# The first slot's first layer, moved from the start of the expert part into the tail of attention

## The chip, the cores and the metric

The kernel runs on one core of a Trainium2 chip. TensorE (PE) multiplies, with PEld as its weight load; VectorE (DVE), ScalarE (ACT) and GpSimd (POOL) do elementwise work, GpSimd also the gathers and scatters by index; SyncE (SP) issues the other transfers. The metric is the time of one execution on the device in microseconds, the median of three runs for the kernel before.

## The reference

Attention over 4 batches and 8 heads of 576 positions with 64 features, causal, mixed by a gate g per head with a read of a memory. Its result, as 2304 tokens of 512 features, goes through a layer of 8 experts, of which each token takes the one with the highest logit:

```
scores = q @ k.T / 8, masked causally;  a = softmax(scores);  local = a @ v
q_p = phi(q);  mem_out = (q_p @ M_prev) / (q_p . z_prev + 1e-6)
x = g * mem_out + (1 - g) * local          # 2304 tokens x 512
e = argmax(x @ w_gate);  w = softmax(x @ w_gate)[e]
out = w * (relu(x @ w1[e]) @ w2[e])        # w1: 512 x 1024, w2: 1024 x 512, 8 experts
```

## The kernel before

**Attention.** The work is cut into 16 units (two heads of a batch each) and every unit into steps: maxima (`n`), scores (`s`), local sums (`p`), the memory read (`m`, `d`), assembling the rows (`a`). Each step has a time in units, from the table `K`, with a shift of its own in `K["sh"]`; `at` and `add` put the steps into a list, the list is sorted by time and the steps are written out in that order (end of `attention`, L944 to L973). A scheduler puts the instructions into each engine's queue from there. The weights of expert 0 and 1 are loaded and cut into two fp16 halves (`Wh`, `Wl`, high and low part, scaled by 64) during attention, each in 8 units of 512 KB. Finished rows go to `x_scratch` in memory, each with its gate value behind it.

**The tail.** When the logits are there, `routing(0)` and `routing(1)` (the steps of `Routing.part`) compute for each token its expert and its rank in it. A slot is 128 tokens of one expert, or half a slot 64; the slots of all experts follow each other, and the table `tab` (TensorE, L1140 and L1155) has for each of them the list of its tokens. `fin1` (L1160, L1161) makes two index tables of it: `idx` for gathers and `ids` for scatters. `busy` (L1067) puts matmuls between the steps whose result nobody reads ("fillers"): four and five of 512 columns, and 46 of 64 columns at the end of `tokens` (`wt`, `wu`, `w3` in `K`). `early_x` gathers the rows of slot 0, which is called the early slot, already in the tail, cuts them into high and low halves and turns them into `rout.xT`.

**The experts.** All engines meet (L1838) and enter a part whose order and semaphores are written by hand. POOL issues the gather of slot 1 (L1490, semaphore `g0`), SP issues the eight loads of the next expert to be staged (L1384), TensorE computes the early slot's first layer (`first_part`, L1582: two halves of 48 matmuls, into the PSUM tiles `m_ph`) and then its second layer (`second_part`, L1598). The rows of slot 1 are cut on VectorE (L1761, L1763), turned on TensorE (L1671) and copied by ScalarE (L1726) and VectorE (L1769). From slot 2 on the rows are turned by SP with transposing transfers: `xtrans` (L1411) issues two of them, for the high and the low half, and VectorE copies the result (L1794). After that the engines run loops over experts and slots: blocks `F0` to `F2` (whole slots) and `H0` to `H2` (half slots) on TensorE, `act_body` and `dve_body` beside them; the weights of later experts are loaded and cut in between. The counts that decide the loops come from VectorE (L1171 to L1177, semaphore `cn`).

The lines of SP at the start of the experts:

```
for u in range(8):
    load(1, u)
...
SP.wait_ge(S["cn"], 7)
...
    SP.dma_start_transpose(out=xB[:, j], in_=xn[j])   # xtrans, after waits for xc, xh, xl
```

Of the kernel before, what the change touches and what calls it, by code (L numbers as in the profile page):

```python
# [17 lines left out]
K = dict(wa=(6, 0, 2, 0, 0, 1, 1, 1, 1, 1, 2, 0, 3, 0, 1, 1, 1, 1, 0, 0, 1, 0, 0), d=3.648, wt=4, wu=5, wv=0, w3=46,  # L18
         sz=(2.207, 2.265, 2.085, 2.03), cr=-1.987, cast1=-0.91, tk1=-0.345, phi0=0.603, pt0=1.592, x0=(19.192,
         19.398), s0=(1.627, 2.3), s1=(1.023, 1.757), p0=(1.742, 3.247), n1=(-0.782, -1.174), n2=(0.27, 0.743),  # L20
         p1=(1.918, 3.326), wd=(8, 8), nc1=0, pact=11, wact=0, pact1=2, wact1=0, nc3=0, cuts=((1, 2), (0, 0)),
         rc=7.857, r0=(15.971, 18.058), r1=(19.098, 21.477), ap=(17.292, 17.456), al=(17.639, 18.974), at=(19.203,
         20.025), k1=-1.514, setup=1.819, v1=2.195, sw=(2.949, 3.089, 3.067, 3.361), sm=(3.958, 3.522, 3.566),
         cast=-0.886, castd=0.004, tk=-0.422, tq=-0.437, phi=0.504, pt=2.11, lk=-1.843, lq=-1.872, lv=0.681,
         n=(-0.15, 0.75), s=(1.05, 2.002), p=(2.014, 3.031), m0=(4.286, 4.261), m7=(2.592, 3.425), m=(2.535, 3.7),
         a0=(4.4, 4.897), a=(4, 5.2), wl=(14.447, 14.278, 15.631, 16.029, 16.835, 17.2, 17.2, 17.976), wc=(15.676,
         17.041, 15.78, 17.231, 17.473, 16.982, 18.21, 17.972), sh=dict(m_steps1w=0.41, wconv01=0.05,
         s_steps14w=0.24, a_steps4=1.03, const_q1=2.08, n_first68=0.16, first_q2=0.12, m_steps2w=0.08,
         p_steps2w=0.15, wload03=-0.02, wconv03=-1.21, s_first12=0.52, setup=-0.73, n_steps4=-0.15, s_steps6w=-0.51,
         p_steps0=0.1, s_steps13=-0.07, phi21=1.31, wload06=0.31, s_steps8w=0.79, wload10=0.62, load6k=-0.33,  # L30
         s_steps4=-0.04, setup_w0=-0.1, n_steps15=-0.7, n_steps13=0.15, n_steps2w=-0.23, load5q=0.27,
# [1193 lines left out]
def experts(nc, tc, es, x_dram, mem, rout, w1, w2, out):  # L1225
# [29 lines left out]
    with tc.tile_critical():  # L1255
# [165 lines left out]
        for u in range(8):  # L1421
            load(1, u)
# [419 lines left out]
```

## Time and profile before

| | kernel before |
|---|---|
| median of three runs | 496.48 us (496.2 to 498.18) |
| the profiled execution, its own time | 493.86 us |
| its span, first to last instruction | 492.1 us |
| granted TensorE clock, mean (1 is 2.4 GHz, 0.5 is 1.2 GHz) | 0.988 |
| TensorE busy, matmuls | 459.1 us (93%) |
| VectorE, ScalarE, GpSimd busy | 355.0, 221.3, 213.4 us |
| chain that ended last, by engine | PE 64%, DVE 12%, SP's queue 8%, DMA 6%, issue 5% |

The three runs and the profiled execution are different executions: durations are read from the profiled one, and a sum over them is compared with its 493.86. In the profile's rows the line is that of the source; "out<-in" are the buffers; a bracket behind a row gives how long the engine stood idle ahead of it and what ended that. In the windows "0.30 (x5)" is busy time with the number of instructions. "issue" is time in which an engine waited for nothing that the profile shows.

### The profile page before, as it was taken

The page shows a single profiled execution, that of the slowest core. Times are in us where ns is not written, and L with a number is a line of the kernel's source. Part 1 is how long each engine was busy: PE and PEld are TensorE (multiplying, and loading weights), DVE is VectorE, ACT ScalarE, POOL GpSimd, SP SyncE. Part 2 cuts the span into 40 slices and gives each one's busy share as a digit, 9 for nine tenths or more (in the row PEclk, how much of TensorE's full clock was granted, in tenths as well). Part 3 has the DMA queues.
Part 4 walks back from the last instruction along what each step waited for, and adds up shares of the span by engine and source line. Part 5 has one row for each costly group of instructions (what it writes and reads, how often), then busy time and mean ns, then how long its engine had stood idle before and what let it go on. Part 6 is the DMA issues. An engine that isn't in the chain of part 4 may idle for free.

```text
span 492.1 us, 14309 instructions
## 1 busy us (share of the span) xinstructions
PE 459.1 (93%) x5279; PEld 314.1 (64%) x5280; DVE 355.0 (72%) x785; ACT 221.3 (45%) x361; POOL 213.4 (43%) x396
## 2 busy tenths in 40 slices
PE   2999899999999989999978999999999989999885
PEld 1555456666666646657656777676677767777864
DVE  2788489786869647989885778788843489844682
ACT  3788565556666655457610444433300163300701
POOL 6567657367748344656331423132232122232132
PEclk9999799999999999999989999999999999999999
DMA  5667979999899989885247999799973199963232
GB/s 119 137 119 158 182 158 172 174 193 228 175 161 164 272 164 191 183 177 209 65 135 286 253 332 254 231 261 305 274 182 98 45 256 304 318 139 90 57 73 69
DMA packets 170106, 90.57 MB, mean 184 GB/s; under 512 B 151471, under 2 KB 152751, under 8 KB 170032
## 3 DMA queue, kind: packets, MB, share of 16 engines
q1 hardware_dynamic: 166192, 77.95, 67.8%
q0 software_dynamic: 3840, 11.80, 7.8%
q8 instruction: 26, 0.43, 0.3%
q14 instruction: 48, 0.39, 0.3%
HBM read 55.35 MB, written 11.60 MB: 136 GB/s over the span
## 4 chain that ended last, share of the span: by engine, by line
PE 64%; DVE 12%; SPq 8%; DMA 6%; issue 5%; ACT 2%; POOL 1%; DVEq 1%; POOLq 0%; ACTq 0%
PE m_ph L1582 18%; PE m_py L1598 16%; PE o L565 7%; PE st L491 5%; SPq L275 3%; PE loc L677 3%; PE sm L596 3%; PE sn L404 2%; SPq L277 2%; DMA m_xB<-m_xn 2%; DMA QT<-mem 1%; DVE mem L1276 1%; PE wm L882 1%; DVE m_w L1276 1%; PE sn L421 1%
## 5 line engine op out<-in xcount | busy, mean ns | idle before, releaser
L1582 PEld LDWEIGHTS m_ph<-m_xT,mem 128*128 128x128 f16 x1344 | 66.0, 98 | 5.9 <-issue 3.3
L1582 PE MATMUL m_ph<-m_xT,mem 128*128 128x128 f16 (+1 forms) x1344 | 67.1, 212 | 2.6 <-DVE m_xT L1794 2.6
L1711 ACT ACTIVATE m_y<-m_py 128x512 f32<-128x512 f32 x17 | 10.2, 597 | 121.6 <-PE m_py L1598 121.6
L510 ACT ACTIVATE aT<-st 128x512 f32<-128x512 f32 x96 | 55.2, 594 | 17.6 <-PE st L491 17.1
L412 DVE TENSOR_REDUCE mt<-sn 128x1 f32<-128x512 f32 (+4 forms) x83 | 54.2, 663 | 12.2 <-PE sn L410 10.0
L495 POOL TENSOR_SCALAR_AFFINE_SELECT aT<-aT 128x128 f32<-128x128 f32 (+2 forms) x160 | 48.0, 317 | 31.9 <-ACT aT L510 29.9
L1598 PE MATMUL m_py<-mem,m_hT 128*128 128x512 f16 x264 | 58.9, 379 | 1.8 <-DVE m_hT L1751 1.8
L565 PE MATMUL o<-aT,mem 128*64 128x320 f32 (+4 forms) x320 | 59.2, 433 | 0.0
L1751 DVE TENSOR_SCALAR m_hT<-m_ph 128x512 f16<-128x512 f32 (+1 forms) x46 | 29.0, 631 | 38.5 <-PE m_ph L1582 37.3
L1538 POOL COPY m_ig<-r_idx 128x1 int32 x22 | 4.0, 184 | 112.9 <-DVE m_xn L1783 111.8
L491 PE MATMUL st<-mem 128*128 128x64 f16 (+6 forms) x224 | 46.8, 262 | 0.4 <-ACT aL L532 0.2
L1598 PEld LDWEIGHTS m_py<-mem,m_hT 128*128 128x128 f16 x264 | 25.3, 98 | 30.3 <-issue 2.0
L491 PEld LDWEIGHTS <-mem 128*128 128x128 f16 (+1 forms) x448 | 32.9, 99 | 16.3 <-issue 4.4
L1582 PEld LDWEIGHTS m_ph<-m_xT,m_w 128*128 128x128 f16 x768 | 40.9, 98 | 3.1 <-issue 1.1
L491 PE MATMUL st<-QT,mem 66*128 66x64 f16 (+6 forms) x224 | 42.3, 262 | 0.4 <-ACT QT L455 0.4
L1582 PE MATMUL m_ph<-m_xT,m_w 128*128 128x128 f16 (+1 forms) x768 | 41.8, 216 | 0.9 <-issue 0.7
L1598 PE MATMUL m_py<-m_w,m_hT 128*128 128x512 f16 x168 | 37.4, 379 | 0.0
L565 PEld LDWEIGHTS o<-aT,mem 128*64 128x64 f32 x320 | 25.3, 137 | 16.7 <-issue 9.8
L1504 POOL DMA_INDIRECT out_dram<-m_y,m_is x23 | 27.2, 1184 | 19.9 <-POOL m_is L1510 19.9
L404 PE MATMUL sn<-mem 128*128 128x128 f16 (+3 forms) x158 | 31.2, 275 | 1.5 <-DVE mt L412 1.1
L1490 POOL DMA_INDIRECT m_xg<-x_scratch,m_ig x22 | 24.0, 1089 | 17.5 <-POOL m_ig L1538 17.5
L1753 DVE SCALAR_TENSOR_TENSOR m_hT<-m_ph,m_hT 128x512 f16<-128x512 f32 (+1 forms) x46 | 29.1, 633 | 1.6
(259 smaller groups left out, 904.2 us busy)
## 6 DMA issues: line engine op xcount, KB each, us to landing
mem<-in_moe_w_dram SPq DMA_DIRECT2D x40, 512.0 KB, 6.1
m_stage<-in_moe_w_dram SPq DMA_DIRECT2D x24, 512.0 KB, 6.6
mem<-in_k_dram SPq DMA_DIRECT2D x32, 128.0 KB, 3.0
mem<-in_q_dram SPq DMA_DIRECT2D x32, 128.0 KB, 2.8
mem<-in_v_dram SPq DMA_DIRECT2D x32, 128.0 KB, 2.8
x_scratch<-xb SPq DMA_DIRECT2D x3, 1152.0 KB, 5.9
mem<-mem SPq DMA_DIRECT2D x6, 288.0 KB, 4.1
x_scratch<-xb SPq DMA_DIRECT2D x1, 864.0 KB, 3.8
```

The costliest lines, as they stand in the source:

```text
L404: nc.tensor.matmul(ps[:, c:c + k1 - k0], QT[:, 5 * hh + t, :], keys(hh)[:, k0:k1], start=(c == 0), stop=(k1 == parts[-1][3] and hh == part ...
L412: nc.vector.reduce_max(out, v, axis=AX.X)
L491: nc.tensor.matmul(ps[:, c:c + n], kk[:, kb, :], qq[:, w:w + n], start=(first and i == 0 and j == 0), stop=(last and i == 1 and j == len(p ...
L495: nc.gpsimd.affine_select(out=ap, in_=ap, pattern=pattern, compare_op=ALU.is_ge, fill=0.0, base=base, channel_multiplier=-1)
L510: nc.scalar.activation(out=a, in_=ps, func=AF.Exp, scale=ESC)
L565: nc.tensor.matmul(o[64 * hh:64 * hh + 64, q0:q0 + n], vv, aa, start=(j == 0), stop=(j == 4), skip_group_check=True)
L1490: G.indirect_dma_start(out=x.rearrange("p h e -> p (h e)"), out_offset=None, in_=x_dram, in_offset=bass.IndirectOffsetOnAxis(ap=i, axis=0) ...
L1504: G.indirect_dma_start(out=out, out_offset=bass.IndirectOffsetOnAxis(ap=i, axis=0), in_=ysb[:, j], in_offset=None, bounds_check=bound, oob ...
L1582: mm = PE.matmul(ph[i2][:, f, 0:N], w[:, kc, c:c + 128], x[:, j, kc, 0:N], start=(i == 0), stop=(i == 11), skip_group_check=True)
L1598: mm = PE.matmul(py, hh, ww[:, 4 + ff // 2, c:c + 512], start=st, stop=sp_)
L1751: V.tensor_scalar(out=hT[i2][0][:, :, 0:N], in0=ph[i2][:, :, 0:N], scalar1=0.0, scalar2=None, op0=ALU.max).then_inc(S[hi], 1)
L1753: V.scalar_tensor_tensor(out=hT[i2][1][:, :, 0:N], in0=ph[i2][:, :, 0:N], scalar=0.0, in1=hT[i2][0][:, :, 0:N], op0=ALU.max, op1=ALU.subtr ...
```

## The change

Slot 0's first layer leaves the expert part and becomes a step `early_p` of attention's list: 24 chunks of four matmuls each, with the times `K["e0"]`. Its result stays in two tiles of a PSUM pool `rout.acc` that both parts now use. At the start of the expert part ScalarE takes the high half (with relu) and VectorE the low half; TensorE goes straight to the second layer. SyncE waits for slot 1's gather before it issues the eight loads. `fin1` makes only one column for that gather and the table `ids`; `idx` is made from it on GpSimd, behind the gather. The 46 fillers go from `tokens` to the start of attention (`fill`), the five at L1144 fall away (`wu=0`), and a block "room" of 48 matmuls is put into TensorE's program, entered only if `er`, which starts at 1, is under 1. `K` gets new times nearly everywhere. The core of the diff:

```diff
-K = dict(wa=(...), d=3.648, wt=4, wu=5, wv=0, w3=46,
-         ... x0=(19.192, 19.398), ... r0=(15.971, 18.058), r1=(19.098, 21.477), ...
+K = dict(wa=(...), d=3.668, wt=4, wu=0, wv=0, w3=46, room=48,
+         ... x0=(19.233, 19.268), e0=(19.944, 21.6), ... r0=(15.971, 18.056), r1=(19.042, 22.191), ...
...
+    def fill(n):
+        for _ in range(n):
+            nc.tensor.matmul(wm[0][:, 0, 0:64], ident16, ident16[:, 0:64], start=True, stop=True)
...
+    at(-1.995, fill, K["w3"])
...
+        def early_p(i):
+            Wh, Wl = W[0]
+            got = []
+
+            def chunk(i2, f, w, j, first, last):
+                def f_():
+                    if first:
+                        got.append(rout.acc.tile([128, 4, 128], F32, tag="acc", name=f"ph{i2}", bufs=2))
+                        rout.ph = got
+                    c = 512 * i2 + 128 * f
+                    for kc in range(4):
+                        nc.tensor.matmul(got[i2][:, f], w[:, kc, c:c + 128], rout.xT[:, j, kc], start=(first and kc == 0),
+                                         stop=(last and kc == 3), skip_group_check=True)
+                return f_
+
+            todo = []
+            for i2 in range(2):
+                q = [(f, w, 0) for f in range(4) for w in (Wh, Wl)] + [(f, Wh, 1) for f in range(4)]
+                todo += [chunk(i2, f, w, j, k == 0, k == 11) for k, (f, w, j) in enumerate(q)]
+            return todo
...
         add(early_x, 0, 4, *K["x0"])
+        add(early_p, 0, 24, *K["e0"])
...
-            busy(K["w3"], 64)
 
         def fin1():
-            V.tensor_scalar(out=s.idx[:, 0:NS], in0=s.tab[0], scalar1=-1.0, scalar2=2304.0, op0=ALU.min, op1=ALU.add)
+            V.tensor_scalar(out=s.i1, in0=s.tab[0][:, 1:2], scalar1=-1.0, scalar2=2304.0, op0=ALU.min, op1=ALU.add)
             V.tensor_scalar(out=s.ids[:, 0:NS], in0=s.tab[0], scalar1=2304.0, scalar2=None, op0=ALU.add)
...
-    ph = [pp.tile([128, 4, 128], F32, name=f"m_ph{i}") for i in range(2)]
+    ph = rout.ph
...
+        SP.wait_ge(S["g0"], 16)
         for u in range(8):
             load(1, u)
...
-        gather("g0", xg0, idx[:, 1:2])
+        gather("g0", xg0, rout.i1)
+        G.tensor_scalar(out=idx, in0=ids, scalar1=2303, scalar2=None, op0=ALU.min).then_inc(S["ix"], 1)
...
+        G.wait_ge(S["ix"], 1)
         G.wait_ge(S["cn"], 7)
...
-        for i2 in range(2):
-            first_part(i2, 128, *W[0], rout.xT).then_inc(S[f"q{i2}"], 1)
         PE.wait_ge(S["q0hi"], 1)
         second_part(0, 0, 0, 128, *W[0])
...
         with block("Z"):
+            PE.br_lt(er, 1, on_true="room", on_false="H0")
+        with block("room"):
+            for _ in range(K["room"]):
+                PE.matmul(py[:, 0:64], rout.ident16, rout.ident16[:, 0:64], start=True, stop=True)
             PE.br("H0")
...
+        for i2 in range(2):
+            A.activation(out=hT[i2][0], in_=ph[i2], func=AF.Relu).then_inc(S[f"q{i2}hi"], 1)
...
-        relu(0, 128, once, "q0hi", "q0lo")
+        for i2 in range(2):
+            V.wait_ge(S[f"q{i2}hi"], 1)
+            V.scalar_tensor_tensor(out=hT[i2][1], in0=ph[i2], scalar=0.0, in1=hT[i2][0],
+                                   op0=ALU.max, op1=ALU.subtract).then_inc(S[f"q{i2}lo"], 1)
```

How the instructions stand, at three places. The first is TensorE's queue in the tail. `r_pr` is the count of the ranks, `r_tab` the table, `r_warm` a filler, `mem_60` the turned rows of the early slot, `mem_59` the weights of expert 0. Before:

```order
L1088 MATMUL r_pr<-r_less,r_ones 128x8
L1088 MATMUL r_pr<-r_ohs,r_ones 128x8
L1067 LDWEIGHTS r_ones
L1067 MATMUL r_warm<-r_ones 128x512
...
L1155 LDWEIGHTS aT
L1155 MATMUL r_tab<-aT 128x144
...
L1067 MATMUL r_warm<-r_ones 128x64
...
L1838 UNCONDITIONAL_BRANCH
L1582 MATMUL m_ph_4122<-mem_60,mem_59 128x128 x48
L1582 MATMUL m_ph_4123<-mem_60,mem_59 128x128 x48
L1598 MATMUL m_py<-mem_59,m_hT_4109 128x512 x8
```

and now:

```order
L1114 MATMUL r_pr<-r_less,r_ones 128x8
L1114 MATMUL r_pr<-r_ohs,r_ones 128x8
L984 LDWEIGHTS mem_59
L984 MATMUL ph_4020<-mem_60,mem_59 128x128
...
L984 MATMUL ph_4113<-mem_60,mem_59 128x128
L1181 LDWEIGHTS aT
L1181 MATMUL r_tab<-aT 128x144
...
L984 LDWEIGHTS mem_59
L984 MATMUL ph_4113<-mem_60,mem_59 128x128
```

The fillers between the counts and the table, and those behind it, are gone; in their places stand matmuls of the early slot's first layer (`ph_4020` is its first half, `ph_4113` its second): 36 between the counts and the table, 28 behind it. 32 more stand ahead of these counts. The two rows of 48 matmuls behind the crossing are no longer there.

The second is POOL's queue from the crossing into the expert part on; `r_idx` and `r_ids` are the index tables, `r_i_70` the new column. Before:

```order
L1838 UNCONDITIONAL_BRANCH
L1490 DMA m_xg_4103<-x_scratch,r_idx 128x576
L1551 TENSOR_LOAD r_cnt
L1552 REGISTER_ALU
L1553 UNCONDITIONAL_BRANCH
L1553 ISA
L1553 COMPARE_AND_BRANCH
L1501 ISA
L1538 COPY m_ig<-r_idx 128x1
```

and now:

```order
L1874 UNCONDITIONAL_BRANCH
L1516 DMA m_xg_4199<-x_scratch,r_i_70 128x576
L1520 TENSOR_SCALAR r_idx<-r_ids 128x145
L1579 TENSOR_LOAD r_cnt
L1580 REGISTER_ALU
L1581 UNCONDITIONAL_BRANCH
L1581 ISA
L1581 COMPARE_AND_BRANCH
```

The table is made directly behind the gather and ahead of the loading of the counts.

The third is VectorE's queue in the maxima of the second unit, early in attention. `sn` are scores in PSUM, `mt` their maxima, `wg_sw` the gating weights in another order, `gm` and `gl` the gates; L436 to L440 before, L435 to L439 after, end the unit's maxima, and the transpose of SyncE for that unit follows them. Before:

```order
L412 TENSOR_REDUCE mt_122<-sn 128x2 x2
L427 TENSOR_REDUCE mt_122<-sn 128x1
L428 TENSOR_REDUCE mt_122<-sn_411 128x1
L412 TENSOR_REDUCE mt_122<-sn 128x1
L181 TENSOR_SCALAR gm<-bt 128x8
L182 TENSOR_SCALAR gl<-bt 128x8
L412 TENSOR_REDUCE mt_122<-sn 128x1
L185 COPY wg_sw<-wg_sb 128x4x7
L186 COPY wg_sw<-wg_sb 128x4
L436 TENSOR_TENSOR mt_122<-mt_122 128x9
```

and now:

```order
L411 TENSOR_REDUCE mt_126<-sn 128x2 x2
L427 TENSOR_REDUCE mt_126<-sn_457 128x1
L184 COPY wg_sw<-wg_sb 128x4x7
L185 COPY wg_sw<-wg_sb 128x4
L191 COPY IW<-wg_sw 64x4x8 x2
L205 COPY early<-wg_sw 64x4x8
L426 TENSOR_REDUCE mt_126<-sn 128x1
L411 TENSOR_REDUCE mt_126<-sn 128x1
L205 COPY early<-wg_sw 64x4x8
```

The copies of the gating weights have moved ahead of maxima which they stood behind.

## Rows read from the trace of the kernel before

**Rows 1.** Windows, two parts: length, busy us (count) by engine, PEclk, DMA share, GB/s

```profile
core 0: us, PE busy (x) PEld busy (x) DVE busy (x) ACT busy (x) POOL busy (x), PEclk, DMA share, GB/s
26.00:246.00 220.00, 212.32 (x2182) 132.00 (x2182) 171.33 (x475) 135.34 (x242) 129.97 (x276) 0.98 0.86 176
246.00:260.00 14.00, 10.03 (x97) 7.02 (x96) 10.66 (x41) 1.98 (x6) 4.23 (x7) 0.88 0.37 120
```

**Rows 2.** Chain that ended last, 240 to 275 us: start, length, engine and line

```profile
254.76 2.04 PE r_warm L1067 x5
256.80 0.60 PE r_tab L1155 x5
257.40 1.82 PE r_warm L1067 x46
259.22 1.33 issue
260.55 5.52 PE m_ph L1582 x96
```

**Rows 3.** Timeline, 236 to 272 us: start, length, engine; idle before in brackets

```profile
260.31 4.03 SPq L1384 DMA_DIRECT2D mem<-in_moe_w_dram  x8
...
260.57 1.03 POOL L1490 DMA_INDIRECT m_xg<-x_scratch,r_idx  x1 [6.63 <-issue]
...
266.81 0.49 DVE L1761 TENSOR_SCALAR m_xn<-m_xg 128x512 f16<-128x512 f32 x1 [1.97 <-DMA m_xg<-x_scratch,r_idx]
...
269.75 0.69 DVE L1769 CAST m_xT<-m_px 128x512 f16<-128x512 f32 x1 [0.34 <-ACT m_xT L1726]
...
271.35 1.24 SPq L1411 DMA_TRANSPOSE m_xB<-m_xn  x1
```

**Rows 4.** DMA issues, the two gathers: queue, count, us from issue to landing

```profile
q<-x_scratch,r_i POOLq DMA_INDIRECT x1, 3.7
m_xg<-x_scratch,r_idx POOLq DMA_INDIRECT x1, 6.2
```

**Rows 5.** Timeline of PE, 271 to 330 us: first layer of slots 1, 2

```profile
271.54 5.52 PE L1582 MATMUL m_ph<-m_xT,mem 128*128 128x128 f16 x96
...
282.08 5.52 PE L1582 MATMUL m_ph<-m_xT,mem 128*128 128x128 f16 x96
```

**Rows 6.** Windows round three holes of PE: before the hole or in it, behind it

```profile
50.00:51.80 1.80, 0.12 (x10) 0.00 (x0) 0.00 (x0) 0.60 (x1) 1.04 (x1) 1.00 0.97 187
...
53.40:60.20 6.80, 6.80 (x29) 2.34 (x29) 3.79 (x4) 4.34 (x6) 5.09 (x4) 0.50 1.06 165
252.70:254.70 2.00, 0.30 (x5) 0.22 (x4) 1.94 (x12) 0.25 (x1) 1.16 (x2) 1.00 0.13 36
254.70:258.20 3.50, 3.50 (x30) 2.21 (x29) 2.31 (x12) 0.90 (x4) 0.00 (x0) 0.51 0.41 105
...
394.00:396.00 2.00, 0.91 (x18) 0.67 (x13) 1.23 (x2) 2.00 (x3) 1.04 (x1) 1.00 0.62 188
```

**Rows 7.** Line L1384, its first eight loads

```profile
DMA to landing us min/median/max: 3.3/7.3/11.2
```

**Rows 8.** DMA packets by size, 271.4 to 273.4 us, then 273.4 to 277

```profile
DMA packets 404, 0.78 MB, mean 391 GB/s; under 512 B 22, under 2 KB 22, under 8 KB 404
...
DMA packets 1308, 0.78 MB, mean 216 GB/s; under 512 B 1121, under 2 KB 1121, under 8 KB 1308
```

**Rows 9.** Windows at the end of the first transposes

```profile
276.50:277.00 0.50, 0.50 (x12) 0.50 (x9) 0.46 (x1) 0.00 (x0) 0.50 (x1) 1.00 0.34 131
```

**Rows 10.** Chain that ended last, 300 to 492 us: a transpose in quiet time

```profile
390.23 1.21 SPq L1411
...
394.77 0.64 DVE m_xT L1794
```

**Rows 11.** Timeline of DVE, 22 to 37 us: a maximum and a copy

```profile
28.34 0.69 DVE L427 TENSOR_REDUCE mt<-sn 128x1 f32<-128x512 f32 x1 [1.01 <-PE sn L426]
...
30.86 1.18 DVE L185 COPY wg_sw<-wg_sb 128x28 f32<-128x28 f32 x1
```

**Rows 12.** Timeline of PE, 301 to 321 us: a stop inside an expert block

```profile
318.83 1.57 PE L1582 MATMUL m_ph<-m_xT,m_w 128*128 128x128 f16 x25 [0.71 <-issue]
```

More of the change, by code (lines that the diff above doesn't have):

```diff
@@ L73 @@
 SW = 64.0
 emitted = []
-TUNE = ["r1", "at", "ap", "al", "x0"]
+TUNE = ["r1", "at", "ap", "al", "x0", "e0"]
 def weight_unit(w1, w2, p, u):
@@ L549, in start @@
         def start():
-            T["o", u] = ps_1.tile([128, 512], F32, tag="acc", name="o", bufs=2)
+            T["o", u] = rout.acc.tile([128, 512], F32, tag="acc", name="o", bufs=2)
             T["oT", u] = ob.tile([128, 576], F32, tag="oT", name="oT")
@@ L584, in sstart @@
         def sstart():
-            T["sm", g] = ps_1.tile([128, 512], F32, tag="acc", name="sm", bufs=2)
+            T["sm", g] = rout.acc.tile([128, 512], F32, tag="acc", name="sm", bufs=2)
             T["sT", g] = ob.tile([128, 576], F32, tag="sT", name="sT", bufs=2)
@@ L1003, in __init__ @@
         s.i0 = rt.tile([128, 1], I32, name="r_i0")
+        s.i1 = rt.tile([128, 1], I32, name="r_i1")
         s.m0 = rt.tile([128, 1], F32, name="r_m0")
@@ L1020, in consts @@
         kp(G.memset(s.cnt[:, NE:], 0))
-        kp(G.memset(s.idx[:, NS:NS + 1], 2303))
         kp(G.memset(s.ids[:, NS:NS + 1], 2304))
-        ii = s.idx[:, 0:NS]
+        ii = s.ids[:, 0:NS]
         it = s.tmp
@@ L1258, in experts @@
                    "ya", "gg", "g0", "cn", "fx", "px", "sc0", "sc1", "pa", "icp", "iscp", "chi", "clo",
-                   "q0", "q1", "q0hi", "q0lo", "q1hi", "q1lo", "qy"):
+                   "ix", "q0hi", "q0lo", "q1hi", "q1lo", "qy"):
             sems[nm] = es.enter_context(nc.semaphore("m_" + nm))
@@ L1667, in experts, with turned @@
         second_part(0, 1, 0, 128, *W[0])
-        for j in range(2):
+        PE.wait_ge(S["q1hi"], 1)
+        second_part(1, 0, 0, 128, *W[0])
+        def turned(j):
             PE.wait_ge(S["fx"], j + 1)
@@ L1744, in experts @@
             cs[k]().then_inc(S["cn"], 1)
-        rv = R(V, [(0, 1), (1, 1), (0, 16), (16, 16)])
-        V.memset(ysb[:, 1], 0.0)
         def relu(i2, N, w, hi, lo):
@@ L1764, in experts @@
                                op0=ALU.mult, op1=ALU.subtract).then_inc(S["fx"], 1)
-        relu(1, 128, once, "q1hi", "q1lo")
+        V.memset(ysb[:, 1], 0.0)
         rv.start()
@@ L1810, in fused @@
         rout.x_dram = x_dram
+        rout.acc = es.enter_context(tc.tile_pool(name="a_acc", bufs=2, space=PSUM))
         rout.xT = mem[1][:, 3456:3968].bitcast(F16).rearrange("p (j k c) -> p j k c", j=2, k=4)
```

118 lines of the change are left out of this document (58 added, 60 removed).

## The prediction, made before the kernel was run

> **What bounds the kernel now.** I read the windows first, for how full TensorE is in each part, then the chain that ended last, then the timeline where the chain leaves TensorE, then the transfers. In the attention part TensorE works 212.32 of 220 us, and in the last 14 us before the expert part only 10.03, at a granted clock of 0.88 [rows 1]. So a reordering of attention has little idle time to win, and the seam between the two parts has much. At the seam the reader should see three things. First, TensorE itself ends the attention part: after five fillers (2.04 us) and the five table matmuls (0.60) come 46 small fillers (1.82), and only after them the 1.33 us of the common crossing into the expert part [rows 2]. Second, the first layer of the early slot, 96 matmuls, takes 5.52 us right behind the crossing [rows 2]. Third, the gather for slot 1 is issued at 260.57 and its data are first used at 266.81, where VectorE had waited 1.97 us for it [rows 3]. It landed 6.2 us after its issue; a gather of the same size in quiet time landed after 3.7 [rows 4]. Eight weight loads were issued from 260.31, just ahead of it [rows 3]. Slot 1 starts on TensorE at 271.54 and slot 2 at 282.08, 10.54 us a slot, 5.52 of it first layer and 5.02 second [rows 5].
>
> **The first layer in the tail.** Its first 32 matmuls stand where TensorE now waits for the routing (0.30 us busy of 2.0 [rows 6]): free. From 254.76 on, TensorE runs 36 more, the five table matmuls, and 28 more, against fillers, table and fillers before. At 5.52/96 = 0.0575 us each, 36 take 2.07 and 28 take 1.61; the table matmuls, which ran at a granted clock of 0.51 [rows 6], I take at half of 0.60. The end is 254.76 + 2.07 + 0.30 + 1.61 = 258.74 instead of 259.22: 0.5 us sooner. Were all 64 at half clock, they would take 7.4 and the end come 3.2 us later; I take the full clock, because the 32 matmuls fill the stretch ahead of it. The 5.52 us behind the crossing go. What is late next is the gather.
>
> **The gather without the loads.** Issued at 260.1 and landing after 3.7 us (bounds 3.7 and 6.2 [rows 4]; 3.7 because nothing is in flight beside it), it is there at 263.8 instead of 266.8. The table that it needs is now one column, so VectorE is not in its way; the full table is made on GpSimd behind it, in the flight of that gather. From the first use of the gathered rows to the end of the cast that slot 1 waits for were 266.81 to 270.44, 3.63 us [rows 3]; slot 1 could start at 267.5, 4.0 us sooner. The second layer of the early slot, 5.02 us, is covered by the flight of the gather; its two activations on ScalarE and two subtractions on VectorE too. If that cover went, it would cost the old order's time back, not more.
>
> **The added wait.** SyncE now waits for the gather with the eight loads behind it, and behind these the two transposes that turn slot 2's rows. The loads start at 263.8 instead of 260.31, 3.5 us later. The last of them lands 11.2 us after its issue [rows 7], so they are a queue of transfers, not eight short ones. The transposes go behind them: issued at 271.35 [rows 3], they show almost no small packets until 273.4 (22, against 1121 in the 3.6 us after) [rows 8], and the transfers end at about 276.8 [rows 9]. In quiet time issue to use took 4.54 us [rows 10], which here would have been 275.9. Before, VectorE was not ready for them any sooner. Now all of this moves by 3.5: the end of the transposes to 280.3, with the copy of 0.64 [rows 10] to 280.9, slot 2 to 281.0. Slot 1 is done at 267.5 + 10.54 = 278.0. TensorE would stand still for 3.0 us, and of the 4.0 us only 1.1 remain at slot 2. The bounds are 1.1 (all moves) and 4.0 (the transposes are not held up). That the loads no longer share the engines with the first gather, but do share them with the early slot's stored result, roughly cancels; I take 1.3, near the end where the rows on the queue point. From slot 2 on everything that follows is ordered as before, so the 1.3 stay. The loads of the next expert wait for the first stored result, which comes earlier, and have slack.
>
> **The attention part, in its new order.** The 46 fillers now run near 20 us: 46 x 1.82/46 at the slow clock is 1.8 us, in place of five of 0.41 (2.04/5), beside VectorE's first maxima; uncovered they would cost at most that. Four copies of VectorE, led by one of 1.18 us that stood ahead of the second unit's transpose, now stand where VectorE waited 1.01 us for TensorE [rows 11]. That lets the transpose and all of SyncE's queue behind it go earlier, by 0 to 1.0; I take 0.6, and for the rest of the new order nothing, between a loss of 1.2 (the 1.8 less the 0.6) and a gain of 1.0. The 48 matmuls in the block "room" never run, since the expert counter starts at 1; they only move code.
>
> **Sum.** 1.3 + 0.6 = 1.9 us less. The profiled execution took 493.86 (span 492.1), so 492.0 by it; the median of the three runs is 496.48, which gives 494.6.
>
> **Rivals.** (1) *The transposes aren't held up.* Then slot 2 follows slot 1 directly and 4.0 + 0.6 are won: 491.9. For it speaks that in quiet time they need 4.54 us only; against it the missing small packets [rows 8]. (2) *The slow stretch in attention goes.* At 53.4 to 60.2 us the clock is 0.50, after TensorE was busy 0.12 of 1.8 us [rows 6]. If the earlier SyncE queue fills that hole, 6.8 us at half rate are up to 3.4 us of work: 1.9 + 3.4 less, 491.2. Against it: the transfers which TensorE waits for there keep their order in SyncE's queue. (3) *The other side: the hole ahead of slot 2 halves the clock.* Both holes of about 2 us, 0.12 busy of 1.8 and 0.30 of 2.0, were followed by a clock of about 0.50, for 6.8 and 3.5 us; one with 0.91 of 2.0 was not [rows 6]. A hole of 3.0 us would be followed by slot 2 at 1.2 GHz. Price: half of 3.5 to 6.8, 1.75 to 3.4 us, so 496.3 to 498.0. It decides from 3.8 us at half clock on (1.9/0.5); at the longer price the kernel is slower than before. The Trainium skill, "TensorE: Matmul & The Clock Gate", section "HAM oscillation", describes just such a kernel, in which each wait for a transfer leaves the next piece of work to start cold; by that rule the time would be (3)'s, and the trace agrees in two of the three holes. (4) *The code lies worse.* TensorE's expert blocks have moved in its program, and in one of them it waited 0.71 us for nothing but its own sequence [rows 12]. Once or twice more in each of the seven changes of expert is 5 to 10 us at the very most; I price it, with an attention order that loses, at 2.5 more than before: 499. The Trainium skill, "Runtime: NRT & Kernel Launch", section "Instruction fetch mechanics", says that a taken branch out of the two loaded pages of code has to wait for a fetch; where the blocks lie against such pages no row here shows.
>
> **How the numbers follow.** Forecast 33% (494.6, its own range 493.3 to 495.6), (1) 17%, (2) 15%, (3) 22%, (4) 13%. I count 0.5%, 2.5 us, as the least that a measurement of this kernel tells from no change. Faster by more: (1), (2) and three tenths of the forecast, 0.42. Slower by more: most of (4) and a seventh of (3), 0.15. The rest, 0.43, lies within. The range takes (1) and (2) in with their own spread, and (3) up to its longer price: 490.6 to 497.9.
>
> **What would show it.** The crossing should start near 258.7; the gather's data be used near 263.8; slot 1 start near 267.5 and slot 2 near 281, with 3 us of idle TensorE ahead of it that ends on the transposes. If slot 2 starts before 279, the queue argument is wrong; if the granted clock falls behind that hole, (3) holds; if it stays at 1.00 near 55 us, (2). If the crossing isn't earlier at all, the tail ran at half clock.

## The result, and the profile after

The changed kernel took 503.13 us (median of 4 runs, 501.92 to 503.69), the kernel before 496.34 in the same comparison: a ratio of 1.0137, 95% interval 1.0088 to 1.0186, so 1.4% slower. The forecast was 494.6 with a range up to 497.9. Ratios here and below are to the kernel before on the same chip and leave out executions more than 1.5% above a kernel's fastest.

The profiled execution took 503.69 us, its span is 502.0 against 492.1. The span's 9.9 us are found by going down TensorE's timeline in both traces and noting by how much the same work starts later:

| work | before | after | later by | step |
|---|---|---|---|---|
| TensorE's last matmul ahead of the crossing ends | 259.22 | 262.22 | +3.00 | +3.00 |
| slot 1, first layer | 271.54 | 270.48 | -1.06 | -4.06 |
| slot 1, second layer | 276.90 | 277.80 | +0.90 | +1.96 |
| slot 2, first layer | 282.08 | 287.19 | +5.11 | +4.21 |
| slot 3, first layer | 292.62 | 299.20 | +6.58 | +1.47 |
| slot 9, first layer | 357.04 | 365.55 | +8.51 | +1.93 |
| end of the span | 492.1 | 502.0 | +9.9 | +1.39 |

The seam did what it was to do, and it was given back within two slots. The timeline of the changed kernel from the end of the tail to slot 2 (start, length, engine; in brackets how long the engine stood before and what ended it):

```profile
258.18 2.17 PE L984 MATMUL ph<-mem,mem 128*128 128x128 f16 x36
...
260.49 1.73 PE L984 MATMUL ph<-mem,mem 128*128 128x128 f16 x28
...
263.59 1.04 POOL L1516 DMA_INDIRECT m_xg<-x_scratch,r_i  x1 [6.01 <-issue]
...
264.71 0.60 POOL L1520 TENSOR_SCALAR r_idx<-r_ids 128x145 int32<-128x145 int32 x1
...
267.18 4.57 SPq L1409 DMA_DIRECT2D mem<-in_moe_w_dram  x8
267.19 0.49 DVE L1796 TENSOR_SCALAR m_xn<-m_xg 128x512 f16<-128x512 f32 x1 [1.53 <-DMA m_xg<-x_scratch,r_i]
267.39 1.27 POOL L1516 DMA_INDIRECT m_xg<-x_scratch,m_ig  x1 [0.81 <-POOL m_ig L1565]
...
270.48 5.52 PE L1610 MATMUL ph<-m_xT,mem 128*128 128x128 f16 x96 [0.88 <-DVE m_xT L1804]
...
275.70 0.49 DVE L1815 TENSOR_SCALAR m_xn<-m_xg 128x512 f16<-128x512 f32 x1 [5.36 <-DMA m_xg<-x_scratch,m_ig]
...
276.40 3.18 SPq L1436 DMA_TRANSPOSE m_xB<-m_xn  x2
...
277.80 5.34 PE L1626 MATMUL m_py<-mem,m_hT 128*128 128x512 f16 x24 [1.80 <-DVE m_hT L1785]
...
286.62 0.43 DVE L1829 COPY m_xT<-m_xB 128x1024 f16<-128x1024 f16 x1 [4.65 <-DMA m_xB<-m_xn]
...
287.19 6.99 PE L1610 MATMUL ph<-m_xT,mem 128*128 128x128 f16 x96 [4.05 <-DVE m_xT L1829]
```

The 36 and 28 matmuls of the first layer ran at full clock (2.17 and 1.73 us). Slot 1's gather was issued at 263.59 and first used at 267.19, 3.6 us later, where it had been 6.2 [rows 4]; slot 1 follows at 270.48, 8.26 behind the crossing and not 12.3. But now look at the two issues at 267.18 and 267.39: the eight loads, which waited for that landing, go out 0.2 us ahead of slot 2's gather. VectorE uses that gather's data only at 275.70, 8.3 us after its issue, having stood 5.36 us; behind it in VectorE's queue is slot 1's activation (L1785), and so TensorE stands 1.80 us ahead of slot 1's second layer. The transposes go out at 276.40, and the copy behind them waits for them until 286.62: TensorE stands 4.05 us.

What the transfers did in that time, first the loads' line, then packets by size from 278 to 281 and from 281 to 285.4 us:

```profile
L1409 SPq DMA_DIRECT2D mem<-in_moe_w_dram x8: 357/457/835, 267.2 to 270.9; - x8
...
DMA to landing us min/median/max: 3.3/10.8/12.9
```

```profile
DMA packets 621, 1.20 MB, mean 401 GB/s; under 512 B 36, under 2 KB 36, under 8 KB 621
...
DMA packets 1236, 0.70 MB, mean 160 GB/s; under 512 B 1093, under 2 KB 1093, under 8 KB 1236
```

The slowest load landed 12.9 us after its issue (11.2 before [rows 7]). From 278 to 281 there are 36 small packets, after that 1093: the transposes, issued at 276.40, moved almost nothing until the loads were through, as before [rows 8], only that now TensorE is waiting for them. Behind the stop the clock is at its lower level; the windows of the stop and of the 3.4 us behind it (PEclk is the third number from the end):

```profile
core 0: us, PE busy (x) PEld busy (x) DVE busy (x) ACT busy (x) POOL busy (x), PEclk, DMA share, GB/s
283.10:287.10 4.00, 0.04 (x1) 0.00 (x0) 0.48 (x2) 3.62 (x5) 0.80 (x1) 0.97 1.18 262
286.90:290.30 3.40, 3.10 (x30) 3.14 (x31) 3.29 (x5) 1.07 (x2) 0.00 (x0) 0.50 1.01 406
```

So slot 2's first layer took 6.99 us and not 5.52. Two stops inside expert blocks follow in which TensorE waited for nothing that the profile shows (bracket "issue"), where there was one of 0.71 [rows 12]:

```profile
313.72 2.74 PE L1610 MATMUL ph<-m_xT,mem 128*128 128x128 f16 x46 [1.02 <-issue]
...
325.07 3.85 PE L1610 MATMUL ph<-m_xT,m_w 128*128 128x128 f16 x66 [1.75 <-issue]
```

### The profile page after: what moved, and what is told of

It is laid out like the page before. It is cut to its first block, busy times and chain, and to the rows that moved or that the text cites. A ratio compares the mean times of both kernels' runs of the same rounds, so it can differ in the third digit from the quotient of the medians.

```text
span 502.0 us, 14285 instructions
## 1 busy us (share of the span) xinstructions
PE 460.0 (92%) x5274; PEld 313.3 (62%) x5275; DVE 352.7 (70%) x783; ACT 222.6 (44%) x363; POOL 212.7 (42%) x396
## 4 chain that ended last, share of the span: by engine, by line
PE 62%; DMA 12%; DVE 8%; SPq 7%; issue 5%; ACT 3%; POOL 2%; DVEq 1%; POOLq 0%; ACTq 0%
PE ph L1610 16%; PE m_py L1626 14%; PE o L564 7%; PE st L490 6%; PE sm L595 4%; DMA m_xB<-m_xn 4%; DMA m_xg<-x_scratch,m_ig 2%; SPq L274 2%; PE sn L403 2%; PE loc L676 2%; SPq L276 2%; DMA QT<-mem 2%; DMA mem<-mem 1%; PE wm L881 1%; PE mem L630 1%
## 5 line engine op out<-in xcount | busy, mean ns | idle before, releaser
L1610 PE MATMUL ph<-m_xT,mem 128*128 128x128 f16 (+1 forms) x1344 | 68.7, 214 | 9.8 <-DVE m_xT L1829 7.9
L1610 PEld LDWEIGHTS ph<-m_xT,mem 128*128 128x128 f16 x1344 | 67.2, 99 | 13.7 <-issue 11.8
L564 PE MATMUL o<-aT,mem 128*64 128x448 f32 (+4 forms) x320 | 57.9, 433 | 0.0
L1785 DVE TENSOR_SCALAR m_hT<-ph 128x512 f16<-128x512 f32 (+1 forms) x44 | 27.6, 628 | 36.2 <-PE ph L1610 35.3
L1610 PE MATMUL ph<-m_xT,m_w 128*128 128x128 f16 (+1 forms) x768 | 41.8, 216 | 1.8 <-issue 1.8
L1610 PEld LDWEIGHTS ph<-m_xT,m_w 128*128 128x128 f16 x768 | 41.0, 98 | 3.7 <-issue 2.1
L564 PEld LDWEIGHTS o<-aT,mem 128*64 128x64 f32 x320 | 22.8, 137 | 17.0 <-issue 10.8
L1787 DVE SCALAR_TENSOR_TENSOR m_hT<-ph,m_hT 128x512 f16<-128x512 f32 (+1 forms) x44 | 27.8, 631 | 1.5
```

The lines of the kernel that those rows point to most:

```text
L564: nc.tensor.matmul(o[64 * hh:64 * hh + 64, q0:q0 + n], vv, aa, start=(j == 0), stop=(j == 4), skip_group_check=True)
L1610: mm = PE.matmul(ph[i2][:, f, 0:N], w[:, kc, c:c + 128], x[:, j, kc, 0:N], start=(i == 0), stop=(i == 11), skip_group_check=True)
L1785: V.tensor_scalar(out=hT[i2][0][:, :, 0:N], in0=ph[i2][:, :, 0:N], scalar1=0.0, scalar2=None, op0=ALU.max).then_inc(S[hi], 1)
L1787: V.scalar_tensor_tensor(out=hT[i2][1][:, :, 0:N], in0=ph[i2][:, :, 0:N], scalar=0.0, in1=hT[i2][0][:, :, 0:N], op0=ALU.max, op1=ALU.subtr ...
```

## The experiments

**First: the wait, the place of the code, the times.** `no_wait` takes the wait out of the changed kernel:

```diff
-        SP.wait_ge(S["g0"], 16)
         for u in range(8):
             load(1, u)
```

> The changed kernel without SyncE's wait for slot 1's gather, so that the eight loads start at the crossing again. Theory 1 (the wait pushes the loads, and with them slot 2's gather and transposes, behind slot 1): slot 1's rows come 2.5 us later (6.2 us of flight instead of 3.6) and slot 1 starts near 273 after the crossing at 262.2, but the stops of 1.8 us ahead of slot 1's second layer and 4.0 us ahead of slot 2, and the slow clock behind them (1.5 us), are gone: about 5 us less, near 498.1. Theory 2 (the stops come from slot 1 now being too early for transfers that take their time anyway): a stop of 2 us or more ahead of slot 2 stays, and the time falls by less than 2 us.

Measured: ratio 1.0060 (1.0023 to 1.0096), 3.8 us less than the changed kernel's by the two ratios, with some 3 us either way by their intervals. Slot 1 started 11.5 us behind the crossing, and no stop stood ahead of slot 2. Theory 1 holds, with a smaller gain than expected: TensorE now stands ahead of slot 1 for its rows, and a stop of 2.03 us for nothing that the profile shows came with a slow stretch of its own behind it.

```profile
269.64 0.40 PE L1699 MATMUL m_px<-r_id,m_xn 128*128 128x128 f16 x4 [3.08 <-DVE m_xn L1795]
...
272.00 5.52 PE L1609 MATMUL ph<-m_xT,mem 128*128 128x128 f16 x96 [0.88 <-DVE m_xT L1803]
...
282.54 5.52 PE L1609 MATMUL ph<-m_xT,mem 128*128 128x128 f16 x96
...
318.80 5.47 PE L1609 MATMUL ph<-m_xT,m_w 128*128 128x128 f16 x66 [2.03 <-issue]
```

`b_wait` puts the same wait alone into the kernel before.

```diff
+        SP.wait_ge(S["g0"], 16)
         for u in range(8):
             load(1, u)
```

> The kernel before with nothing but SyncE's wait for slot 1's gather ahead of the eight loads. Theory 1 (the wait costs by itself): the gather lands after 3.7 us instead of 6.2, which slot 1 can use for at most 0.3 us, since TensorE is still in the early slot's second layer; the loads start near 264.4, slot 2's gather and transposes end 4 us later or more, and slot 2 starts near 286 instead of 282.1: 4 to 6 us more than before, 500.3 to 502.3. Theory 2 (the wait costs only together with the early first layer): within 1 us of the kernel before, 495.3 to 497.3.

Measured: 0.9980 (0.9933 to 1.0026); but the median of all its 12 runs, 492.45 to 503.39, is 499.29 against 495.6. By time alone it stays open. The trace shows where the loss would go: slot 2's gather is here issued ahead of the loads, slot 2 is held up by 0.31 us only, but slot 3 by 1.92 for its turned rows, and the third expert by 2.37 for weights that VectorE had cut too late.

```profile
263.48 1.03 POOL L1491 DMA_INDIRECT m_xg<-x_scratch,m_ig  x1 [0.80 <-POOL m_ig L1539]
264.03 4.09 SPq L1384 DMA_DIRECT2D mem<-in_moe_w_dram  x8
...
282.48 5.52 PE L1583 MATMUL m_ph<-m_xT,mem 128*128 128x128 f16 x96 [0.31 <-DVE m_xT L1795]
...
295.10 5.52 PE L1583 MATMUL m_ph<-m_xT,mem 128*128 128x128 f16 x96 [1.92 <-DVE m_xT L1795]
...
318.71 7.15 PE L1583 MATMUL m_ph<-m_xT,m_w 128*128 128x128 f16 x96 [2.37 <-DVE m_w L1276]
```

So in this trace the later loads left slot 2 nearly where it was and showed at slot 3 and at the third expert. Theory 1's price was right at most for a part of the runs, and its place was wrong.

`no_room` empties the block "room" (`room=48` to `room=0`); no other row moves in any queue.

> The changed kernel with the block of 48 matmuls that never run left empty; nothing else moves in any queue. Theory 1 (the two stops of TensorE inside expert blocks, 1.02 and 1.75 us against one of 0.71 before, hang on where the blocks lie): the stops change places or sizes, 1 to 3 us less in sum. Theory 2 (they hang on the traffic of the moment): the same two stops at the same blocks, the time within 0.5 us of 503.1.

Measured: 1.0116 (1.0078 to 1.0153). The two stops without a wait were gone, and in their places stood waits for late weights (1.02 us) and for VectorE (1.02 us); the stop ahead of slot 2 was 5.47 us.

```profile
287.37 7.92 PE L1610 MATMUL ph<-m_xT,mem 128*128 128x128 f16 x96 [5.47 <-DVE m_xT L1829]
...
322.57 5.52 PE L1610 MATMUL ph<-m_xT,m_w 128*128 128x128 f16 x96 [1.02 <-DVE m_w L1301]
...
329.11 5.34 PE L1626 MATMUL m_py<-m_w,m_hT 128*128 128x512 f16 x24 [1.02 <-DVE m_hT L1785]
```

Theory 1 was right on the stops and wrong on the gain: beside the late loads, the stops without a wait hid others.

`old_k` gives attention the times of before, fillers and tail as changed.

```diff
-K = dict(wa=(...), d=3.668, ...   # the new times
+K = dict(wa=(...), d=3.648, ...   # those of before; r1, x0, e0, routing1, early_p0w, w3 as changed
```

> The changed kernel with the times that attention's steps had before; only those of the tail (routing 1, early gather, early first layer) and the fillers stay new. Theory 1 (of the 3.2 us by which the logits are later, 1.3 are the 46 fillers, and the rest is the new order, in the stops near 183 and 206 us): the logits' last matmuls start near 245.1 instead of 247.05, 1.9 us less in all, near 501.2. Theory 2 (the new order is as good, and the rest comes from the accumulators' shared pool or the fillers): the logits stay within 0.5 us of 247.

Measured: 1.0247 (1.0204 to 1.0290), the logits' last matmuls at 249.1, 2 us later than in the changed kernel and not 1.9 sooner. The fillers had been scheduled elsewhere (at 6.0 us and not near 20), with TensorE at half clock from 10.1 to 23.8 us behind them. The times belong to the fillers; nothing is told on either alone.

**Second: the moved layer alone.** `early_only` keeps the moved layer and its tail, and has attention's TensorE order exactly as before, no fillers, an empty room, no wait, and both index tables on VectorE. `early_wait` is the same with the wait.

```diff
-         wt=4, wu=0, w3=46, room=48, ...
+         wt=4, wu=0, w3=0, room=0, ...       # attention's times of before
-        SP.wait_ge(S["g0"], 16)                # early_wait keeps this line
-        G.tensor_scalar(out=idx, in0=ids, ...)
+            V.tensor_scalar(out=s.idx[:, 0:NS], in0=s.tab[0], ...)   # in fin1, last
```

> The changed kernel with the attention order of before (same times, no fillers at the start, an empty block room), no wait of SyncE, and the gather table made on VectorE behind the new column; of the change, the moved first layer and what goes with it in the tail stay. Theory 1 (the moved layer is worth about what the tail frees, and all losses come from wait, fillers and times): crossing near 258.9, slot 1 some 11.5 us behind it, near 270.5, and slot 2 near 281.0, against 271.5 and 282.1 before: about 1 us less than before, 494.6. Theory 2 (the faster start of the experts collides with the loads by itself): a stop of over 1 us ahead of slot 2 or 3, and no gain or a loss against before.

> The same kernel as early_only with SyncE's wait for slot 1's gather. Theory 1 (the wait makes the gather 2.5 us faster and moves the loads back by 3.6 us; slot 1 then outruns the transposes behind the loads): slot 1 near 267.3, a stop of 3 us or more ahead of slot 2, which starts near 283, with the clock at half behind it: 2 to 4 us more than early_only. Theory 2 (what stopped slot 2 in the changed kernel was its gather behind the loads, since the table was made on GpSimd between the two gathers): with the table on VectorE slot 2's gather goes ahead of the loads, the stop is under 1.5 us, and the time is within 1 us of early_only.

Measured: 1.0272 (1.0231 to 1.0313) and 1.0256 (1.0186 to 1.0326), 13 us above before. `early_wait` had the stop ahead of slot 2 that its theory 1 named (2.92 us, half clock behind it), but took no more time than `early_only`. Slot 1 (12.0 us behind the crossing) and slot 2 (22.5) of `early_only` were near what was expected, the crossing (260.88) 2 us later; the loss stood far behind, in stops of 2.7 and 4.3 us in the expert blocks, with 35 code loads in the execution and not 26. That is why runs further down move nothing but the code.

```profile
308.03 6.43 PE L1610 MATMUL ph<-m_xT,mem 128*128 128x128 f16 x83 [2.69 <-issue]
...
471.15 7.73 PE L1610 MATMUL ph<-m_xT,mem 128*128 128x128 f16 x96 [4.28 <-DVE mem L1304]
```

`idx_v` makes the gather table on VectorE in the changed kernel, so that slot 2's gather goes out sooner; `no_fill` takes the 46 fillers out of it (`w3=46` to `w3=0`, after which the scheduler moves other rows too).

> The changed kernel with the gather table made on VectorE, behind the new column, as before the change, and not on GpSimd between the first two gathers; the wait stays. Theory 1 (the order of slot 2's gather and the loads decides): that gather is issued some 0.7 us sooner, ahead of the loads, and lands after 4 to 5 us and not 8.3; the stop ahead of slot 1's second layer (1.8 us) goes; the one ahead of slot 2 stays, since the transposes stand behind the loads in any case, and shrinks by 1 us at most: 1 to 2 us less than 503.1. Theory 2 (the loads alone decide): slot 2's gather lands no sooner, no change within 0.5 us.

> The changed kernel without the 46 fillers at the start of attention; the scheduler moves a few instructions around the place with them. Theory 1 (they take 1.3 us of TensorE with nothing beside them to hide it): the logits' last matmuls start 1.3 us sooner, near 245.7 instead of 247.0, and the time is 1.3 us less. Theory 2 (they keep the granted clock up or fill a wait): no change within 0.5 us, or a stretch at half clock between 8 and 30 us that costs as much or more.

Measured: `idx_v` 1.0150 (1.0107 to 1.0192), no gain that the time tells. In its trace the gather goes out 0.5 us ahead of the loads, its data are used after 4.9 us and not 8.3, and the stop ahead of slot 1's second layer is gone. The transposes go out 2.9 us sooner than in the changed kernel, and TensorE still stands 4.09 us for them:

```profile
266.94 1.03 POOL L1518 DMA_INDIRECT m_xg<-x_scratch,m_ig  x1 [0.80 <-POOL m_ig L1566]
267.43 4.66 SPq L1411 DMA_DIRECT2D mem<-in_moe_w_dram  x8
...
271.86 0.49 DVE L1815 TENSOR_SCALAR m_xn<-m_xg 128x512 f16<-128x512 f32 x1 [1.22 <-DMA m_xg<-x_scratch,m_ig]
...
273.55 6.74 SPq L1438 DMA_TRANSPOSE m_xB<-m_xn  x2
...
276.14 5.34 PE L1626 MATMUL m_py<-mem,m_hT 128*128 128x512 f16 x24
...
285.01 0.43 DVE L1829 COPY m_xT<-m_xB 128x1024 f16<-128x1024 f16 x1 [6.11 <-DMA m_xB<-m_xn]
...
285.58 7.15 PE L1610 MATMUL ph<-m_xT,mem 128*128 128x128 f16 x96 [4.09 <-DVE m_xT L1829]
```

Theory 1 holds for the trace: measured from the crossing (262.53), slot 2 starts at 23.05 and not at 24.97, so the late gather cost 1.9 us at slot 2, which is the stop ahead of slot 1's second layer; the stop ahead of slot 2 stays with the loads. That these 1.9 us can't be seen in the time is within the two intervals. `no_fill` 1.0115 (1.0061 to 1.0170): not told apart from the changed kernel; its logits came later, not sooner.

**Third: the place of the code alone.** `b_shift` is the kernel before with a block that never runs, so that by the count of instructions (no view of the profile gives addresses) its expert blocks lie where those of the changed kernel lie; `b_179` has the same block with 37 matmuls.

```diff
         with block("Z"):
+            PE.br_lt(er, 1, on_true="room", on_false="H0")
+        with block("room"):
+            for _ in range(85):                    # b_179: 37
+                PE.matmul(py[:, 0:64], rout.ident16, rout.ident16[:, 0:64], start=True, stop=True)
             PE.br("H0")
```

> The kernel before with nothing but a block of 85 matmuls that never run, so that TensorE's expert blocks lie where they lie in the changed kernel. Theory 1 (where the blocks lie decides over the stops): stops of about 1 us and 1.8 us without any wait appear in the blocks of the second and third expert, as in the changed kernel, 1 to 3 us more than before. Theory 2 (only the change's transfers make them): one stop of 0.7 us as before, the time within 1 us.

> The kernel before with 37 matmuls in a block that never runs, so that by the count of instructions its expert blocks lie where they lie in early_66 and in no_room. Theory 1 (this place is good for any kernel): stops without a wait under 0.5 us, and the time within 1 us of before. Theory 2 (the count alone does not tell the place): stops and code loads in the last 50 us as in b_shift, 5 us or more above before.

Measured: `b_shift` 1.0226 (1.0170 to 1.0281), `b_179` 1.0033 (1.0001 to 1.0066). Eighty-five matmuls that never run cost 11 us. The trace shows it as code loads: in the last 48 us the instruction queue moved 10 blocks of 16 KB in `b_shift`, and from 455 us on one in the kernel before. The loads of these two stretches, then three of TensorE's stops in `b_shift`, two of them in its last 48 us, and a window behind the second:

```profile
q8 instruction: 10, 0.16, 1.7%
```

```profile
q8 instruction: 1, 0.02, 0.2%
```

```profile
308.66 3.62 PE L1582 MATMUL m_ph<-m_xT,mem 128*128 128x128 f16 x35 [3.43 <-issue]
...
471.45 2.72 PE L1582 MATMUL m_ph<-m_xT,mem 128*128 128x128 f16 x24 [4.03 <-DVE mem L1276]
...
494.44 4.96 PE L1582 MATMUL m_ph<-m_xT,mem 128*128 128x64 f16 x90 [1.85 <-issue]
```

```profile
469.50:476.20 6.70, 4.41 (x41) 4.28 (x42) 4.62 (x6) 4.24 (x6) 1.01 (x2) 0.50 0.14 28
```

It stood 4.03 us for weights that were cut late, 1.85 and 3.43 for nothing that the profile shows, with the lower clock behind them. The branch at the head of the block isn't the cause: `b_179` has it too. `b_179` stood for 0.98 and 1.50 us without a wait, against theory 1, but its time and its 26 loads are near those of before. The Trainium skill, "Runtime: NRT & Kernel Launch", section "Instruction fetch mechanics", says that a taken branch out of the loaded pages waits for a fetch of its page; the trace agrees, in that one load lies in the 3.5 us ahead of the row at 308.66. Whether a place is good could not be read from the count of instructions: by it, `early_28` (`room=28`) puts `early_only`'s blocks where they lie in the kernel before, `early_66` (`room=66`) where they lie in `no_room`; `early_28w` is `early_28` with the wait.

> The kernel early_only with 28 matmuls in the block room, which never run, so that TensorE's expert blocks lie where they lie in the kernel before. Theory 1 (the stops of 2.7, 4.3 and 2.1 us in early_only come from code that has to be loaded, and hang on where the blocks lie): they shrink to under 1.2 us each, the slow clock behind them goes with them, and the time falls by 8 to 12 us, to 496 to 500; what is left is the moved layer's own worth. Theory 2 (they come from the transfers of the moved layer's kernel): the stops stay, 508 within 1 us.

> The same with SyncE's wait for slot 1's gather. Theory 1 (the wait moves the loads, and the transposes behind them, to after slot 1's end): a stop of about 3 us ahead of slot 2, then half clock: 3 to 4 us more than early_28. Theory 2 (the loads have slack, and the faster gather is worth as much): within 1 us of early_28.

> The kernel early_only with 66 matmuls in the block room, so that TensorE's expert blocks lie where they lay in the run without the room, which showed no stop that waited for nothing. Theory 1 (the place decides): no such stop over 0.5 us, and a time at or below that of early_28. Theory 2: stops as in early_28 or more.

Measured: `early_28` 1.0250 (1.0194 to 1.0306) and `early_28w` 1.0261 (1.0206 to 1.0316), 35 code loads each; `early_66` 0.9993 (0.9958 to 1.0027), with 26. `early_66` differs from `early_only` by 66 matmuls that never run, and by 2.8% of its time, though one stop of 1.03 us without a wait is left in it. Beside the bad place the wait costs nothing that the time tells, in `early_28w` as in `early_wait`, though a stop of 2.85 us stands ahead of slot 2. At the good place the moved layer by itself is worth nothing that the time tells.

**Fourth: the wait at a good place.** `early_66w` is `early_66` with the wait. `early_66i` waits only for the issue of the gather; `after_i` is the changed kernel with that wait and an empty room, `after_i48` with the room at 48, `no_wait0` the changed kernel with neither wait nor room.

```diff
-        SP.wait_ge(S["g0"], 16)
+        SP.wait_ge(S["gi"], 1)
...
         gather("g0", xg0, rout.i1)
+        G.sem_inc(S["gi"], 1)
```

> The kernel early_66 (moved first layer, attention order of before, good place of the code) with SyncE's wait for the landing of slot 1's gather: the wait's own price at a good place. Theory 1 (transposes stand behind the later loads): a stop of about 3 us ahead of slot 2, and 2 to 4 us more than early_66. Theory 2 (the stop of 2.9 us ahead of slot 1, which the wait takes away, is worth as much): within 1 us of early_66.

> The kernel early_66 with SyncE waiting only until GpSimd has issued slot 1's gather, not until it has landed: the loads start 1.4 us later than in early_66 and 2.5 us sooner than with the whole wait. Theory 1 (it is enough that the gather's packets go first): slot 1 starts 8 us behind the crossing and not 12, the stop ahead of slot 2 is under 1 us, 2 to 3 us less than early_66 and about 2 us less than before. Theory 2 (the gather shares the engines with the loads all the same): it lands 5 us or more after its issue, and the time is that of early_66 within 1 us.

> The changed kernel with the wait for the gather's issue in place of its landing, and with the block room empty, as in no_room. Theory 1 (wait and place of the code are what the change lost, beside some 2 us in attention): slot 1 some 8 us behind the crossing, no stop over 1.5 us ahead of slot 2, 497 to 499. Theory 2 (slot 2's gather, which goes behind the loads here too, and the weights that come later hold up slot 2 or the third expert): a stop of 3 us or more, 500 or more.

> The kernel after_i with the block room back at 48 matmuls: of the changed kernel only the wait differs (issue, not landing). Theory 1 (the wait costs most, the place of the code little between these two): a ratio within 0.4% of after_i's 0.994. Theory 2 (the place costs as much): TensorE's stops of 1.0 and 1.8 us without a wait are back, and the ratio is 1.000 to 1.006.

> The changed kernel without SyncE's wait and with an empty block room. Theory 1 (without the wait the gather shares with the loads and slot 1 starts some 12 us behind the crossing): the ratio is that of no_wait, 1.006, less what the place gives, 0.998 to 1.004, and above after_i's 0.994. Theory 2 (the wait in any form gives nothing, the place all): the same as after_i within 0.3%.

Measured, the ratios to before (the changed kernel's own 1.0137 is the one at top left):

| | landing wait | wait for the issue | no wait |
|---|---|---|---|
| changed kernel, room 48 | 1.0137 | 1.0047 (1.0015 to 1.0080) | 1.0060 |
| changed kernel, room empty | 1.0116 | 0.9943 (0.9913 to 0.9972) | 1.0001 (0.9969 to 1.0033) |
| early_66 | 1.0046 (1.0016 to 1.0075) | 0.9990 (0.9954 to 1.0026) | 0.9993 |

In each row the wait for the landing has the highest ratio, by 0.5 to 1.7%. `early_66w` and `early_66i` were measured in the same comparison (medians 500.5 and 496.89 us over 12 runs each), and so were `after_i48` and `no_wait0` (499.02 and 496.32), which differ by the room; the other pairs come from different ones. The wait for the issue did not do what it was made for: in `after_i` the loads still go out ahead of the gather, 1.2 us behind the crossing, which is when they go without any wait, and slot 1 starts 10.1 us behind the crossing and not 8.

```profile
263.32 4.22 SPq L1409 DMA_DIRECT2D mem<-in_moe_w_dram  x8
...
263.50 1.04 POOL L1516 DMA_INDIRECT m_xg<-x_scratch,r_i  x1 [5.99 <-issue]
```

So the two right columns are the same kernel as far as the order of the transfers goes; that the middle row stands at 0.994 and 1.000 is then what two comparisons can differ by, and of the differences above this leaves the sign, which is the same in all three rows, and not the size. Without wait and room the changed kernel is about as fast as the kernel before; whether it beats it stays open. In the bottom row the trace shows the trade. Without the wait (first row) TensorE stands for slot 1's rows, with it for slot 2's transposes:

```profile
269.82 0.40 PE L1700 MATMUL m_px<-r_id,m_xn 128*128 128x128 f16 x4 [2.93 <-DVE m_xn L1796]
```

```profile
264.47 3.99 SPq L1412 DMA_DIRECT2D mem<-in_moe_w_dram  x8
...
270.59 6.08 SPq L1439 DMA_TRANSPOSE m_xB<-m_xn  x2
...
282.19 0.43 DVE L1830 COPY m_xT<-m_xB 128x1024 f16<-128x1024 f16 x1 [6.13 <-DMA m_xB<-m_xn]
...
282.76 7.93 PE L1611 MATMUL ph<-m_xT,mem 128*128 128x128 f16 x96 [4.10 <-DVE m_xT L1830]
```

In these two executions the trade comes out even, 499.34 us without the wait and 498.83 with it: the price is in the medians, not in the traces.

## Why the prediction was wrong

**The first layer in the tail: right.** From the five fillers' place to the crossing nothing was lost and little won: the tail from the logits' last matmuls on took 15.2 us and not 15.6, 0.4 sooner against 0.5 forecast, with the 64 matmuls at full clock. A slow stretch stands in the tail as before, now at 249.3 to 252.8 in place of 254.8 to 258.2. TensorE was busy for all of the 3.3 us ahead of it, so the former hole is not what set it off; what did isn't shown.

**The gather without the loads: right.** 3.6 us against 3.7; slot 1 8.26 us behind the crossing against 8.76 (267.5 less 258.74).

**The added wait: the step that failed.** It moved the loads and the transposes behind them by 3.5 us and took 1.3 us as the gain left at slot 2. Measured from the crossing, slot 2 started at 24.97 (22.3 forecast, 22.86 before). Apart from attention, which put the logits 3.4 us later, slot 2 started 1.7 us later than before, where 1.3 sooner was forecast. The end of the transposes is where it went wrong: their rows were copied at 286.62, 24.4 us behind the crossing, where 21.6 was forecast (280.3 less 258.74). Of these 2.8 us the larger part is slot 2's gather, which fell behind the loads, since the table made on GpSimd put its issue after them; the prediction named the table and held it to be hidden, and looked for no second gather. In `idx_v`, where that gather goes first, the copy stands at 22.5 and slot 2 at 23.05. The rest isn't taken apart further; the loads went out 3.9 us later against the crossing, not 3.5, and were slower by up to 1.7. `idx_v` still stands 4.09 us for the transposes, as the queue argument said. For the whole kernel the sign of the term was wrong: by the ratios the wait costs 0.5% at a good place, and 0.8% in the changed kernel.

**The clock behind the stop: the rival (3), and it should have been in the sum.** The forecast itself had a stop of 3.0 us, and its rows showed two of three shorter ones followed by half clock; a stop of 4.0 was, for 1.47 us more, a little less than the 1.75 priced. It is a chance and no certainty: a stop of 3.08 us ahead of slot 1 was followed by full clock in `no_wait` (first layer 5.52 us) and by half clock in `early_28` (7.47).

**Attention: the sign was wrong.** 0.6 us less were forecast. The logits' last matmuls, before and in the changed kernel:

```profile
243.66 2.38 PE L750 MATMUL lg<-IW,oT 128*128 128x16 f32 x20
```

```profile
247.05 2.38 PE L749 MATMUL lg<-IW,oT 128*128 128x16 f32 x20
```

They start 3.4 us later, of which the tail gives back 0.4. One execution says little here. In six profiles with the new order (the changed kernel, `no_wait`, `no_room`, `idx_v`, `after_i`, `no_wait0`) the crossing began at 262.2, 260.5, 261.1, 262.5, 262.1 and 261.5, mean 261.7; in four with the order of before (`b_wait`, `b_shift` and `b_179` with it) at 259.2, 259.1, 260.2 and 260.2, mean 259.7. That is 2.0 us later; a seventh profile, `after_i48`, began at 260.5 and brings it to 1.8. But this is not the price of the new order alone: in the seven `early_` kernels, which have the order of before, no fillers and the moved layer, the crossing began between 259.3 and 261.0, mean 260.1. Some 1.4 to 1.6 us are left for the new times and the fillers, no more than the spread of such a group. The 46 fillers, which were priced at 1.8 at most if uncovered, stood in three groups for 1.3 us in all with TensorE full on both sides. That they are the cause isn't shown: without them nothing was won, and in `no_fill` the logits came at 248.68.

**The place of the code: the right mechanism, its price open here and far higher elsewhere.** Rival (4) had 2.5 us and 13%. Place alone moved the kernel before by 11 us, and `early_only` by 14. In the changed kernel the room gives away 1.0 and 1.75 us of stops, some of which cover late weights: emptying it gave 0.2% with the landing wait, which is within the intervals, and 0.6 to 1.0% without. The number of code loads doesn't tell these stops: it is 26 in the changed kernel, in `no_room` and before.

**Rivals (1) and (2)** did not come: the transposes were held up in every run with the landing wait, and the granted clock was 0.50 from 54.8 to 61.6 us in the changed kernel, as in the one before from 53.4 to 60.2.

## What to carry to other kernels

A wait that clears the way for one transfer moves every transfer behind it in that queue, and those that other queues now issue behind it: follow each of them to its first user, and put the slow clock behind a stop that you forecast into the sum. Ahead of any comparison of two kernels with loops in their code, count the code loads in the trace, and look for stops without a wait even where the counts agree: here a kernel was 2% slower for where its blocks lie, and then no edit could be judged beside it. Where two edits hide each other's stops, take both away before you price either.

## What the runs showed of the hardware that was not expected

Eighty-five matmuls that never run cost 11 us (code loads from 26 to 36 in the execution), 37 cost 0.3%, and by the count of instructions ahead of the blocks the same place was a good one in one kernel (before) and a bad one in another (`early_28`, 35 loads). A transpose by transfer, issued 10 to 12 us ahead of its use, moved almost nothing until loads issued ahead of it were through, while the data of a gather issued 0.5 us ahead of the same loads were used after 4.9 us, and those of one issued 0.2 us behind them after 8.3. An increment put behind a gather on GpSimd let the waiting engine go before the profile shows the gather's start (263.32 and 263.50).
